# Decode attention beside a gated MLP: 28 rows of w_down summed by VectorE ahead of the last V

## The chip, the core and the metric

One NeuronCore of a Trainium2 chip runs the whole program. TensorE (PE) multiplies, VectorE (DVE) and ScalarE (ACT) work on tiles in SBUF and PSUM, GpSimd (POOL) makes two constants, and SyncE (SP) issues nearly all loads. The metric is the device time of one execution in microseconds; lower is better.

## The reference

One token passes through a block in which attention over a cache and a gated MLP stand side by side. The input x has 576 features, the cache 32 heads of 16384 positions with 128 features, the MLP 4608 inner features; all is in 32-bit floats.

```python
xn = _layernorm(x)
q = (xn @ wq)                                  # 32 heads of 128
scores = einsum("bhqd,bhkd->bhqk", q, k_cache) * (Dh ** -0.5)
o = einsum("bhqk,bhkd->bhqd", softmax(scores), v_cache)
attn = o.reshape(B, Sq, H * Dh) @ wo           # 4096 x 576
h = gelu(xn @ w_gate) * (xn @ w_up)            # tanh form of gelu
out = x + attn + h @ w_down                    # 4608 x 576
```

Each number of the caches and weights is used once. The caches alone are 2 x 32 x 8.39 MB.

## The kernel before

**Memory.** Three slots of SBUF, A, B and C, hold 64 KB in each of 128 partitions, so one slot takes one head's K or V (8.39 MB; a partition holds 128 positions). At the start the slots hold the weights w_q, w_gate and w_up. Later K of the even heads goes to B, K of the odd heads to A, and V of every head to C. At the end w_down (36 rows of 576 in each partition; "a row" below is 128 x 576 numbers) and w_o (32 such rows) go where room is.

**Order.** Nothing is scheduled by a planner: each engine's program is written out in order, and semaphores join them. `take(engine, s)` waits for a semaphore and lowers it, `give` raises it, `done` makes an engine wait for its own last instruction, and `load` issues a DMA. SP's loads all go to one queue, so a load that waits holds back every later one. fA, fB and fV tell SP that slot A, B or C is free; kA, kB and vL tell the engines that a K or V has landed.

**Stages.** First x is normed, and PE multiplies it with w_q, w_gate and w_up as they arrive; DVE and ACT make the MLP's inner vector hT from it. Then come 32 heads:
- `q_spread` on PE puts the head's q in all partitions; ACT copies it to `qs`.
- DVE (`dve_head`) multiplies the slot of K with qs in place (L188), sums over each 128 features into S (L191), and finds the largest score with PE's help (L193, L195, L370, L372). After L191 it frees the slot. L191 waits for `sf`, which PE gives with its first product on V of the head before, since S must have been read by then.
- ACT makes the exponentials `pe` (L264).
- PE multiplies pe with V in slot C (L377, 32 matmuls), ACT copies the result to `o4`, PE gathers it (L384) and with that frees slot C.

In one turn of SP's loop of heads, K for B, V, K for A and V are issued, each behind its slot's semaphore. Behind the loop the order is written out:

```python
        take(SP, fV)
        load(C, vv[H - 1], vL)
        take(SP, fB)
        load(B[:, : WD_A * D], wdv[:, : WD_A * D], s_tail[0])
        take(SP, fA)
        ...
```

that is V of the last head, 28 rows of w_down into B, its other 8 rows and 20 rows of w_o into A, and the last 12 rows of w_o in pieces of 6, 3, 2 and 1 into C.

**Tail.** `add_out` on PE (L401) adds one row after another into output banks: a row's 128 entries of hT or of the normed heads (`oT`) are the stationary operand, its 576 columns the moving one. Each row is two matmuls of 288 columns, and four of 144 for the last six rows. DVE clears the banks ahead of that (L335) and gives s_mz. After the row before the last six (s_hf) DVE adds the two halves' sums to x (L344, L345), PE adds that in (L429), and after the last row DVE copies the result (L347), which ACT stores.

Of the kernel before, what the change touches and what calls it, by code (L numbers as in the profile page):

```python
# [8 lines left out]
AF = mybir.ActivationFunctionType  # L9
ALU = mybir.AluOpType  # L10
AX = mybir.AxisListType

P = 128
H, SK, DH = 32, 16384, 128
D, DF = 576, 4608
R = SK // P
DJ = 4
DM = P * DJ
SCALE = DH**-0.5
EPS = 1e-5  # L20
HALF = D // 2
QUART = D // 4
# [3 lines left out]
WD_T = DF // P  # L26
FG = DF // 4
FB = (11 * WD_T, 11 * WD_T, 10 * WD_T)
WO_T = HD // P
ROW3 = 3 * DF  # L30
SLOT = R * DH
SLOTS = (28672, 94208, 159744)
LOW, HIGH = 16512, 225280
WD_A, WO_A = 28, 20
WO_C = (6, 3, 2, 1)
WO_Q = 6

# [2 lines left out]
def kernel(ctx: ExitStack, tc: tile.TileContext, x, k_cache, v_cache, wq, wo, wg, wu, wd, out):  # L40
    nc = tc.nc
    PE, DVE, ACT, SP, PL = nc.tensor, nc.vector, nc.scalar, nc.sync, nc.gpsimd
# [3 lines left out]
    def small(name, shape, where="low"):  # L46
        n = 4
        for s in shape[1:]:
            n *= s
        h = nc.alloc_sbuf_tensor_at(name, list(shape), F32, offset=at[where])  # L50
        at[where] += (n + 31) // 32 * 32
        assert at["low"] <= SLOTS[0] and at["high"] <= 229344
        return h.ap()
# [4 lines left out]
    A, B, C = slot("slot_a", 0), slot("slot_b", 1), slot("slot_c", 2)  # L58
# [3 lines left out]
    ones = small("ones", [P, P])  # L62
    x2 = small("x2", [P, HALF])
# [33 lines left out]
    onx = small("onx", [P, P])  # L97
    oT = small("oT", [P, WO_T])
    ot = small("ot", [P, QUART])

    kv = k_cache.rearrange("b h (p n) d -> (b h) p (n d)", p=P)
    vv = v_cache.rearrange("b h (p n) d -> (b h) p (n d)", p=P)
# [9 lines left out]
    def sem(name):  # L112
        return nc.alloc_semaphore(f"{name}_{next(count)}")
# [3 lines left out]
    def take(eng, s, n=1):  # L117
        eng.wait_ge(s, n).then_inc(s, -n)  # L118

    def give(eng, s, n=1):  # L120
        eng.sem_inc(s, n)

    def done(eng, inst):
        s = self_sem.setdefault(id(eng), None) or self_sem.__setitem__(id(eng), sem("own")) or self_sem[id(eng)]
        inst.then_inc(s, 1)
        take(eng, s)

    def load(dst, src, s, eng=None):
        (eng or SP).dma_start(dst, src).then_inc(s, 16)
# [7 lines left out]
    for n in "gu":  # L137
# [13 lines left out]
        sem(n) for n in ("qp", "qd", "qr", "pm", "pt", "nm", "pb", "ex", "sf", "pv", "o4", "pc"))  # L151
    s_al, s_pl, s_on, s_po, s_ot, s_mz, s_hf, s_x4, s_end, s_cp, s_out = (
        sem(n) for n in ("al", "pl", "on", "po", "ot", "mz", "hf", "x4", "end", "cp", "out"))
    s_tail = [sem("tail") for _ in range(3 + len(WO_C))]

    pgb = bank[:3]
    qgb = bank[3:5]
# [23 lines left out]
        take(PE, s_r)  # L181
        PE.matmul(pqb[:, :DH], ones, qh, start=True, stop=True).then_inc(qp, 1)  # L182

    def dve_head(k, slot, s_k, s_f):
        kt = slot.rearrange("p (n d) -> p n d", d=DH)
        take(DVE, s_k, 16)
        take(DVE, qr)
        done(DVE, DVE.tensor_mul(kt, kt, qs.unsqueeze(1).to_broadcast([P, R, DH])))  # L188
        give(DVE, qd)
        take(DVE, sf)  # L190
        done(DVE, DVE.tensor_reduce(S, kt, axis=AX.X, op=ALU.add))  # L191
        give(DVE, s_f)
        DVE.reduce_max(pm, S, axis=AX.X).then_inc(s_pm, 1)  # L193
        take(DVE, s_pt)
        DVE.tensor_reduce(nm, ptb[:1, :P], axis=AX.X, op=ALU.max, negate=True).then_inc(s_nm, 1)  # L195

    with tc.tile_critical(no_gpsimd_drain=True):

        load(wq_t, wmain["q"], s_wq)
        load(qt, wtail["q"], s_qt)  # L200
        for n in "gu":
            load(rows[n], wmain[n][:, ROW3:], s_mix[n])
# [2 lines left out]
        take(SP, fA)  # L205
        load(main["u"], wmain["u"][:, :ROW3], s_main["u"])
        take(SP, fB)
        load(B, kv[0], kB)
        take(SP, fA)
        load(A, kv[1], kA)  # L210
        take(SP, fV)
# [1 line left out]
        with SP.Fori(0, H // 2 - 1) as i:  # L213
            take(SP, fB)
            load(B, kv[bass.ds(2 * i + 2, 1)].rearrange("a p f -> (a p) f"), kB)
            take(SP, fV)
            load(C, vv[bass.ds(2 * i + 1, 1)].rearrange("a p f -> (a p) f"), vL)
            take(SP, fA)
            load(A, kv[bass.ds(2 * i + 3, 1)].rearrange("a p f -> (a p) f"), kA)
            take(SP, fV)  # L220
            load(C, vv[bass.ds(2 * i + 2, 1)].rearrange("a p f -> (a p) f"), vL)
        take(SP, fV)
        load(C, vv[H - 1], vL)
        take(SP, fB)
        load(B[:, : WD_A * D], wdv[:, : WD_A * D], s_tail[0])
        take(SP, fA)
        load(A[:, : (WD_T - WD_A) * D], wdv[:, WD_A * D :], s_tail[1])
        wo_a = (WD_T - WD_A) * D
        load(A[:, wo_a : wo_a + WO_A * D], wov[:, : WO_A * D], s_tail[2])
        take(SP, fV)  # L230
        lo = WO_A
        for k, n in enumerate(WO_C):
            load(C[:, (lo - WO_A) * D : (lo - WO_A + n) * D], wov[:, lo * D : (lo + n) * D], s_tail[3 + k])
            lo += n


        PL.memset(x2, 0.0).then_inc(s_zero, 1)
# [14 lines left out]
        done(ACT, ACT.activation(qs, pqb[:, :DH], AF.Copy))  # L252
        give(ACT, qr)
        give(ACT, s_q0)
        take(ACT, s_t1)
        ACT.activation(th, t1, AF.Tanh, scale=0.7978845608028654).then_inc(s_th, 1)
        with ACT.Fori(0, H) as h:
            q_pick(h + 1)
            take(ACT, qp)
            take(ACT, qd)  # L260
            ACT.activation(qs, pqb[:, :DH], AF.Copy).then_inc(qr, 1)
            take(ACT, s_pb)
            done(ACT, ACT.activation(nb, ptb[:, 256:257], AF.Copy, scale=SCALE))  # L263
            ACT.activation(pe, S, AF.Exp, bias=nb, scale=SCALE, accum_out=lsum[:, bass.ds(h, 1)]).then_inc(s_ex, 1)  # L264
            take(ACT, s_pv)
            ACT.activation(o4, PO, AF.Copy).then_inc(s_o4, 1)  # L266
            take(ACT, s_pc)
            done(ACT, ACT.activation(oall[:, bass.ds(h, 1)], pcb[:, :1], AF.Copy))
# [7 lines left out]
        done(DVE, DVE.memset(ones, 1.0))  # L276
        done(DVE, DVE.memset(eps_t, EPS))
        done(DVE, DVE.memset(whose[:, H:], 0.0))
        take(DVE, s_x, 16)
        for i in range(2):  # L280
            done(DVE, DVE.bn_stats(st[:, i, :], xrow[:, i * HALF : (i + 1) * HALF]))
# [46 lines left out]
        done(DVE, DVE.scalar_tensor_tensor(t2, th, 1.0, g, op0=ALU.add, op1=ALU.mult))  # L328
        done(DVE, DVE.scalar_tensor_tensor(hT, t2, 0.5, u, op0=ALU.mult, op1=ALU.mult))
        give(DVE, s_h)  # L330
        with DVE.Fori(0, H // 2):
            dve_head(0, B, kB, fB)
            dve_head(1, A, kA, fA)
        for z in (*half_b, bank[2]):
            done(DVE, DVE.memset(z, 0.0))  # L335
        give(DVE, s_mz)
# [26 lines left out]
            steps += [(j, main[n][:, j * DF : (j + 1) * DF], [(s_main[n], 16)] if j == 0 else []) for j in range(DJ - 1)]  # L363
            project(steps, FG, FB, pgb, s_pj)
        take(PE, s_q0)
        give(PE, sf)
        with PE.Fori(0, H):
            q_spread()
            take(PE, s_pm)
            PE.transpose(ptb[:1, :P], pm, ident).then_inc(s_pt, 1)  # L370
            take(PE, s_nm)
            PE.matmul(ptb[:, 256:257], ones[:1, :], nm, start=True, stop=True).then_inc(s_pb, 1)  # L372
            take(PE, s_ex)
            take(PE, vL, 16)
            for k in range(32):
                q = 32 * (k % 4)
                i = PE.matmul(PO[q : q + 4, :], pe[:, 4 * k : 4 * k + 4], C[:, k * 512 : (k + 1) * 512],  # L377
                              start=k < 4, stop=k >= 28)
                if k == 0:
                    i.then_inc(sf, 1)  # L380
            i.then_inc(s_pv, 1)
            take(PE, s_o4)
            for j in range(4):
                i = PE.matmul(pcb[:, :1], o4[:, j * DH : (j + 1) * DH], same[:, j : j + 1], start=j == 0, stop=j == 3)  # L384
                if j == 0:
                    i.then_inc(fV, 1)
            i.then_inc(s_pc, 1)
# [10 lines left out]
        def add_out(groups, lhs, w, last=False):  # L398
            n = D // len(groups)
            for k, gr in enumerate(groups):  # L400
                i = PE.matmul(gr, lhs, w[:, k * n : (k + 1) * n], start=id(gr) not in seen, stop=last)  # L401
                seen.add(id(gr))
            return i

        take(PE, s_tail[0], 16)
        for j in range(WD_A):
            add_out(half[j % 2], hT[:, j : j + 1], B[:, j * D : (j + 1) * D])
        take(PE, s_on)
        PE.matmul(bank[5][:, :WO_T], onx, same, start=True, stop=True).then_inc(s_po, 1)
        take(PE, s_tail[1], 16)  # L410
        for j in range(WD_A, WD_T):
            add_out(half[j % 2], hT[:, j : j + 1], A[:, (j - WD_A) * D : (j - WD_A + 1) * D])
        take(PE, s_ot)
        take(PE, s_tail[2], 16)
        ends = [sum(WO_C[:k]) + WO_A for k in range(len(WO_C))]
        for j in range(WO_T):
            if j in ends:
                take(PE, s_tail[3 + ends.index(j)], 16)
            w = A[:, wo_a + j * D : wo_a + (j + 1) * D] if j < WO_A else C[:, (j - WO_A) * D : (j - WO_A + 1) * D]
            if j < WO_T - WO_Q:  # L420
                i = add_out(half[j % 2], oT[:, j : j + 1], w, last=j >= WO_T - WO_Q - 2)
                if j == WO_T - WO_Q - 1:
                    i.then_inc(s_hf, 1)
                continue
            if j == WO_T - 3:
                take(PE, s_x4)
                for k, gr in enumerate(quart):
                    r, lo = 32 * (k // 2), k % 2 * QUART
                    PE.matmul(gr, ones[r : r + 1, :1], x2[r : r + 1, lo : lo + QUART], start=False, stop=False)  # L429
            i = add_out(quart, oT[:, j : j + 1], w, last=j == WO_T - 1)  # L430
        i.then_inc(s_end, 1)

        take(DVE, qr)
# [30 lines left out]
```

## Time and profile before

| | us |
|---|---|
| median of 3 runs | 1384.4 |
| all runs | 1384.4, 1381.16, 1564.85 |
| profiled execution, device time | 1383.64 |
| profiled execution, span of the trace | 1381.9 |
| busy: PE, DVE, ACT | 442.0, 1141.0, 71.5 |
| read from HBM | 587.60 MB, 425 GB/s over the span |

The span runs from the first to the last instruction that the trace shows; the device time is 1.74 us more. All times inside the execution are in microseconds from the start of the span. The longest of the three runs lies far from the other two, and the profiled execution lies with those two.

In the trace's rows, a timeline row has start, duration, engine, line, operation, tiles and count (matmuls that follow each other closely are merged into one row; a float matmul leaves two records), and in brackets the idle time of the engine before it. PEld is PE's load of the stationary operand. SPq and ACTq are the engines' issuing of DMAs. A row of stages gives its window and length, the busy time of PE, PEld, DVE, ACT and POOL with counts, the granted TensorE clock, the share of the DMA engines that was busy, and GB/s. The time from issue to landing is shown for each kind of load.

### The profile page before, as it was taken

Reading aid. Unit: us, or ns where it says so; the run is one execution under the profiler, and the core shown is the slowest. Engines: PE = TensorE matmul, PEld = TensorE weight load, DVE = VectorE, ACT = ScalarE, POOL = GpSimd, SP = SyncE. Lnnn points to the kernel's source line nnn. Section 1 sums busy time; section 2 is a strip of 40 time slices with the busy share of each in tenths; the row PEclk is TensorE's granted clock in tenths of the full one; section 3 lists DMA queues with packets and bytes.
Section 4 is the critical chain, followed back from the end, with each engine's and each line's share of the span. In section 5 each row is a group of like instructions: output and inputs, shape, how many; then the busy total and the mean of one; then the engine's idle time right before and its main releaser. Section 6 shows DMA issues by size and latency. Waiting matters only on the chain. (4 is left out here: it accounts for less than half of the span.)

```text
span 1381.9 us, 8013 instructions
## 1 busy us (share of the span) xinstructions
PE 442.0 (32%) x3104; PEld 171.5 (12%) x3104; DVE 1141.0 (83%) x173; ACT 71.5 (5%) x231; POOL 1.0 (0%) x7
## 2 busy tenths in 40 slices
PE   3531233333322233333332223333332223333336
PEld 1110011101110011111111011111110111111112
DVE  1149999999988998989888898989988899989910
ACT  0000000000000000000000000000000000000000
POOL 0000000000000000000000000000000000000000
PEclk9765565565555556556655665665665566566567
DMA  9999999999999999999999999999999999999697
GB/s 401 435 442 419 435 429 438 425 438 431 436 434 433 438 431 434 438 427 438 434 433 438 431 436 433 433 440 429 436 438 427 438 431 436 436 431 438 258 413 320
DMA packets 11396, 587.70 MB, mean 425 GB/s; under 512 B 1271, under 2 KB 1277, under 8 KB 1662
## 3 DMA queue, kind: packets, MB, share of 16 engines
q1 hardware_dynamic: 11376, 587.60, 98.4%
q8 instruction: 5, 0.08, 0.0%
q10 hardware_dynamic: 14, 0.01, 0.0%
q14 instruction: 1, 0.01, 0.0%
HBM read 587.60 MB, written 0.00 MB: 425 GB/s over the span
## 5 line engine op out<-in xcount | busy, mean ns | idle before, releaser
L377 PE MATMUL bank<-slot_c,pe 128*4 128x512 f32 x2048 | 296.4, 738 | 491.6 <-PEq L118 491.6
L191 DVE TENSOR_REDUCE s<-slot_a 128x128 f32<-128x16384 f32 x16 | 275.5, 17220 | 35.5 <-DVEq L118 35.5
L191 DVE TENSOR_REDUCE s<-slot_b 128x128 f32<-128x16384 f32 x16 | 275.5, 17220 | 31.5 <-DVEq L118 31.5
L188 DVE TENSOR_TENSOR slot_b<-slot_b,qs 128x16384 f32<-128x16384 f32 x16 | 275.6, 17225 | 8.4 <-DVEq L118 8.4
L188 DVE TENSOR_TENSOR slot_a<-slot_a,qs 128x16384 f32<-128x16384 f32 x16 | 275.6, 17226 | 0.0
L377 PEld LDWEIGHTS bank<-slot_c,pe 128*4 128x4 f32 x2048 | 84.7, 99 | 676.2 <-issue 664.5
L370 PE MATMUL bank<-ident,pm 128*1 128x128 f32 x32 | 11.9, 372 | 289.4 <-PEq L118 289.4
L266 ACT ACTIVATE o<-bank 128x512 f32<-128x512 f32 x32 | 19.1, 597 | 761.1 <-ACTq L118 761.1
L384 PE MATMUL bank<-same,o 128*128 128x1 f32 x256 | 32.7, 249 | 28.3 <-PEq L118 28.3
L370 PEld LDWEIGHTS bank<-ident,pm 128*1 128x1 f32 x32 | 2.5, 79 | 296.3 <-issue 296.3
L384 PEld LDWEIGHTS bank<-same,o 128*128 128x128 f32 x256 | 31.0, 191 | 57.1 <-issue 57.1
L182 PE MATMUL bank<-qh,ones 128*128 128x128 f32 x66 | 20.4, 402 | 54.6 <-PEq L118 54.6
L316 DVE TENSOR_TENSOR slot_c<-bank,same 128x396 f32<-128x396 f32 (+1 forms) x6 | 3.3, 558 | 37.1 <-DVEq L118 36.7
L344 DVE TENSOR_TENSOR x<-x,bank 64x288 f32<-64x288 f32 x1 | 0.5, 456 | 35.4 <-DVEq L118 35.4
L195 DVE TENSOR_REDUCE nm<-bank 1x1 f32<-1x128 f32 x32 | 8.9, 279 | 21.5 <-DVEq L118 21.5
L372 PE MATMUL bank<-nm,ones 1*128 1x1 f32 x64 | 17.7, 343 | 18.5 <-PEq L118 18.5
L303 DVE TENSOR_TENSOR slot_c<-bank,same 128x512 f32<-128x512 f32 x2 | 1.4, 692 | 26.1 <-DVEq L118 25.9
L263 ACT ACTIVATE nb<-bank 128x1 f32<-128x1 f32 x32 | 5.5, 171 | 303.3 <-ACTq L118 303.3
L182 PEld LDWEIGHTS bank<-qh,ones 128*128 128x128 f32 x66 | 13.3, 251 | 57.9 <-issue 57.9
L372 PEld LDWEIGHTS bank<-nm,ones 1*128 1x128 f32 x64 | 15.9, 307 | 27.9 <-issue 27.9
L338 DVE RECIPROCAL rl<-bank 128x32 f32<-128x32 f32 x1 | 0.4, 358 | 22.2 <-DVEq L118 22.2
L178 ACT ACTIVATE qh<-qd,whose 128x128 f32<-128x128 f32 x33 | 13.2, 401 | 49.3 <-ACTq L118 49.3
(77 smaller groups left out, 151.2 us busy)
## 6 DMA issues: line engine op xcount, KB each, us to landing
slot_b<-in_B_w_down_dram SPq DMA_DIRECT2D x1, 8064.0 KB, 40.5
slot_b<-in_B_w_gate_dram SPq DMA_DIRECT2D x1, 6912.0 KB, 55.4
slot_a<-in_B_w_up_dram SPq DMA_DIRECT2D x1, 6912.0 KB, 38.8
slot_a<-in_A_wo_dram SPq DMA_DIRECT2D x1, 5760.0 KB, 52.6
slot_c<-in_B_w_gate_dram SPq DMA_DIRECT2D x1, 2304.0 KB, 28.9
slot_c<-in_B_w_up_dram SPq DMA_DIRECT2D x1, 2304.0 KB, 36.0
slot_a<-in_B_w_down_dram SPq DMA_DIRECT2D x1, 2304.0 KB, 38.2
slot_c<-in_A_wo_dram SPq DMA_DIRECT2D x1, 1728.0 KB, 33.4
```

Source lines behind the costliest of these rows:

```text
L178: ACT.activation(qh, qd4.rearrange("p j t -> p (j t)"), AF.Copy, scale=whose[:, bass.ds(h, 1)]).then_inc(s_r, 1)
L182: PE.matmul(pqb[:, :DH], ones, qh, start=True, stop=True).then_inc(qp, 1)
L188: done(DVE, DVE.tensor_mul(kt, kt, qs.unsqueeze(1).to_broadcast([P, R, DH])))
L191: done(DVE, DVE.tensor_reduce(S, kt, axis=AX.X, op=ALU.add))
L195: DVE.tensor_reduce(nm, ptb[:1, :P], axis=AX.X, op=ALU.max, negate=True).then_inc(s_nm, 1)
L263: done(ACT, ACT.activation(nb, ptb[:, 256:257], AF.Copy, scale=SCALE))
L266: ACT.activation(o4, PO, AF.Copy).then_inc(s_o4, 1)
L316: done(DVE, DVE.tensor_mul(gm[:, at_ * WD_T : (at_ + m) * WD_T].rearrange("p (m t) -> p m t", t=WD_T), pgb[b][:, :size].rearrange("p (m t) ...
L370: PE.transpose(ptb[:1, :P], pm, ident).then_inc(s_pt, 1)
L372: PE.matmul(ptb[:, 256:257], ones[:1, :], nm, start=True, stop=True).then_inc(s_pb, 1)
L377: i = PE.matmul(PO[q : q + 4, :], pe[:, 4 * k : 4 * k + 4], C[:, k * 512 : (k + 1) * 512], start=k < 4, stop=k >= 28)
L384: i = PE.matmul(pcb[:, :1], o4[:, j * DH : (j + 1) * DH], same[:, j : j + 1], start=j == 0, stop=j == 3)
```

## The change

There are six edits.

1. `WD_B = 28` rows of w_down are loaded into slot B ahead of V of the last head, no longer behind it.
2. DVE, not PE, works on these rows: after its last head, a loop of 14 turns with two `scalar_tensor_tensor` each adds `B row x hT` to a new tile `acc` (128 x 576), each waiting for the one before. Then it gives `s_sum`, and only then does it clear the output banks and give s_mz. PE adds acc's partitions with one row's worth of matmuls against ones.
3. K of head 0 is loaded in two halves (semaphores `s_k0` and kB), and `dve_head` works on it in two parts. So that head stands ahead of DVE's loop, and the last head behind it.
4. `sf` comes from ACT, after it has made the exponentials, in place of PE's first matmul on V.
5. The first load, of w_q's main part, stands in a `tile_critical` section of its own, and all else in a second one.
6. The 20 rows of w_o in slot A come in pieces of 12 and 8, each with a semaphore; PE walks through a list `pieces`.

```diff
-WD_A, WO_A = 28, 20
+WD_B = 28
+WO_A = (12, 8)
...
+    acc = small("acc", [P, D])
...
+    pieces, at_a, lo = [(A, 0, wdv, WD_B, WD_T - WD_B)], WD_T - WD_B, 0
+    for n in WO_A:
+        pieces.append((A, at_a, wov, lo, n))
+        at_a, lo = at_a + n, lo + n
+    at_c = 0
+    for n in WO_C:
+        pieces.append((C, at_c, wov, lo, n))
+        at_c, lo = at_c + n, lo + n
...
-    def dve_head(k, slot, s_k, s_f):
+    def dve_head(slot, s_k, s_f, parts=1):
...
+        n = R // parts
+        for i in range(parts):
+            blk = kt[:, i * n : (i + 1) * n, :]
+            take(DVE, s_k if i == parts - 1 else s_k0, 16)
+            if i == 0:
+                take(DVE, qr)
+            done(DVE, DVE.tensor_mul(blk, blk, qs.unsqueeze(1).to_broadcast([P, n, DH])))
+            if i == parts - 1:
+                give(DVE, qd)
+            if i == 0:
+                take(DVE, sf)
+            done(DVE, DVE.tensor_reduce(S[:, i * n : (i + 1) * n], blk, axis=AX.X, op=ALU.add))
...
     with tc.tile_critical(no_gpsimd_drain=True):
-
         load(wq_t, wmain["q"], s_wq)
+    with tc.tile_critical(no_gpsimd_drain=True):
+
         load(qt, wtail["q"], s_qt)
...
-            load(B, kv[0], kB)
+            for half_k in range(2):
+                k0 = slice(half_k * SLOT // 2, (half_k + 1) * SLOT // 2)
+                load(B[:, k0], kv[0][:, k0], (s_k0, kB)[half_k])
...
+        take(SP, fB)
+        load(B[:, : WD_B * D], wdv[:, : WD_B * D], s_wd)
         take(SP, fV)
         load(C, vv[H - 1], vL)
-        take(SP, fB)
-        load(B[:, : WD_A * D], wdv[:, : WD_A * D], s_tail[0])
         take(SP, fA)
...
         give(ACT, s_q0)
+        give(ACT, sf)
...
-            ACT.activation(pe, S, AF.Exp, bias=nb, scale=SCALE, accum_out=lsum[:, bass.ds(h, 1)]).then_inc(s_ex, 1)
+            done(ACT, ACT.activation(pe, S, AF.Exp, bias=nb, scale=SCALE, accum_out=lsum[:, bass.ds(h, 1)]))
+            give(ACT, s_ex)
+            give(ACT, sf)
...
+        done(DVE, DVE.memset(acc, 0.0))
...
-        with DVE.Fori(0, H // 2):
-            dve_head(0, B, kB, fB)
-            dve_head(1, A, kA, fA)
+        dve_head(B, kB, fB, 2)
+        with DVE.Fori(0, H // 2 - 1):
+            dve_head(A, kA, fA)
+            dve_head(B, kB, fB)
+        dve_head(A, kA, fA)
+        take(DVE, s_wd, 16)
+        with DVE.Fori(0, WD_B // 2) as i:
+            for k in range(2):
+                done(DVE, DVE.scalar_tensor_tensor(acc, B[:, bass.ds((2 * i + k) * D, D)], hT[:, bass.ds(2 * i + k, 1)], acc,
+                                                   op0=ALU.mult, op1=ALU.add))
+        give(DVE, s_sum)
...
-        give(PE, sf)
...
-                if k == 0:
-                    i.then_inc(sf, 1)
...
+        take(PE, s_sum)
+        add_out(half[1], ones[:, :1], acc)
         take(PE, s_tail[0], 16)
-        for j in range(WD_A):
-            add_out(half[j % 2], hT[:, j : j + 1], B[:, j * D : (j + 1) * D])
+        for j in range(WD_B, WD_T):
+            add_out(half[j % 2], hT[:, j : j + 1], A[:, (j - WD_B) * D : (j - WD_B + 1) * D])
```

SP's program behind its loop of heads, before (slot_c from the V cache is V of the last head):

```order
L129 DMA slot_c<-in_A_v_cache_dram 128x16384
L129 DMA slot_b<-in_B_w_down_dram 128x16128
L129 DMA slot_a<-in_B_w_down_dram 128x4608
L129 DMA slot_a<-in_A_wo_dram 128x11520
L129 DMA slot_c<-in_A_wo_dram 128x3456
```

and SP's program at the same place now:

```order
L131 DMA slot_b<-in_B_w_down_dram 128x16128
L131 DMA slot_c<-in_A_v_cache_dram 128x16384
L131 DMA slot_a<-in_B_w_down_dram 128x4608
L131 DMA slot_a<-in_A_wo_dram 128x6912
L131 DMA slot_a<-in_A_wo_dram 128x4608
L131 DMA slot_c<-in_A_wo_dram 128x3456
```

The load into slot B has moved ahead of V, and w_o's load into slot A has become two.

DVE behind the last head, before (nm is the last head's largest score, bank are the output banks, rl, on and onx norm the heads' outputs):

```order
L195 TENSOR_REDUCE nm<-bank 1x1
L331 REGISTER_ALU
L331 COMPARE_AND_BRANCH
L335 MEMSET bank 128x512 x3
L338 RECIPROCAL rl<-bank 128x32
L339 TENSOR_TENSOR on<-oall,rl 128x32
L340 TENSOR_TENSOR onx<-on,quarter 128x128
```

and DVE at the same place now (ISA rows make addresses from the loop's count):

```order
L212 TENSOR_REDUCE nm<-bank 1x1
L358 UNCONDITIONAL_BRANCH
L358 ISA
L360 REGISTER_ALU
L360 SCALAR_TENSOR_TENSOR acc<-slot_b,hT,acc 128x576
L360 ISA
L360 SCALAR_TENSOR_TENSOR acc<-slot_b,hT,acc 128x576
L358 REGISTER_ALU
L358 COMPARE_AND_BRANCH
L364 MEMSET bank 128x512 x3
L367 RECIPROCAL rl<-bank 128x32
L368 TENSOR_TENSOR on<-oall,rl 128x32
```

The loop over acc stands between the last head and the memsets, so the memsets and the three operations of the norm are behind it.

SP's program at its start now:

```order
L214 NO_OP
L482 UNCONDITIONAL_BRANCH
L131 DMA slot_a<-in_A_wq_dram 128x16384
L214 UNCONDITIONAL_BRANCH
L214 NO_OP
L216 NO_OP
L482 UNCONDITIONAL_BRANCH
L131 DMA slot_b<-in_A_wq_dram 128x2048
```

The first load has the same rows in front of it as before; the four rows behind it, up to the second load, are new.

More of the change, by code (lines that the diff above doesn't have):

```diff
@@ L153 @@
         sem(n) for n in ("al", "pl", "on", "po", "ot", "mz", "hf", "x4", "end", "cp", "out"))
-    s_tail = [sem("tail") for _ in range(3 + len(WO_C))]
+    pieces, at_a, lo = [(A, 0, wdv, WD_B, WD_T - WD_B)], WD_T - WD_B, 0
[6 more added lines that the diff above has]
+        at_c, lo = at_c + n, lo + n
+    s_tail = [sem("tail") for _ in pieces]
+    s_wd, s_sum, s_k0 = sem("wd"), sem("sum"), sem("k0")
     pgb = bank[:3]
@@ L182, in q_spread @@
         PE.matmul(pqb[:, :DH], ones, qh, start=True, stop=True).then_inc(qp, 1)
-    def dve_head(k, slot, s_k, s_f):
+    def dve_head(slot, s_k, s_f, parts=1):
         kt = slot.rearrange("p (n d) -> p n d", d=DH)
[L186 to L191, printed above, removed]
+        n = R // parts
[10 more added lines that the diff above has]
+            done(DVE, DVE.tensor_reduce(S[:, i * n : (i + 1) * n], blk, axis=AX.X, op=ALU.add))
         give(DVE, s_f)
@@ L221 @@
             load(C, vv[bass.ds(2 * i + 2, 1)].rearrange("a p f -> (a p) f"), vL)
+        take(SP, fB)
+        load(B[:, : WD_B * D], wdv[:, : WD_B * D], s_wd)
         take(SP, fV)
         load(C, vv[H - 1], vL)
-        take(SP, fB)
-        load(B[:, : WD_A * D], wdv[:, : WD_A * D], s_tail[0])
         take(SP, fA)
-        load(A[:, : (WD_T - WD_A) * D], wdv[:, WD_A * D :], s_tail[1])
-        wo_a = (WD_T - WD_A) * D
-        load(A[:, wo_a : wo_a + WO_A * D], wov[:, : WO_A * D], s_tail[2])
+        for (t, to, src, lo, n), sm in zip(pieces[:-len(WO_C)], s_tail):
+            load(t[:, to * D : (to + n) * D], src[:, lo * D : (lo + n) * D], sm)
         take(SP, fV)
[L231 to L234, printed above, removed]
+        for (t, to, src, lo, n), sm in list(zip(pieces, s_tail))[-len(WO_C):]:
+            load(t[:, to * D : (to + n) * D], src[:, lo * D : (lo + n) * D], sm)
         PL.memset(x2, 0.0).then_inc(s_zero, 1)
@@ L403, in add_out @@
             return i
+        take(PE, s_sum)
+        add_out(half[1], ones[:, :1], acc)
         take(PE, s_tail[0], 16)
-        for j in range(WD_A):
-            add_out(half[j % 2], hT[:, j : j + 1], B[:, j * D : (j + 1) * D])
+        for j in range(WD_B, WD_T):
+            add_out(half[j % 2], hT[:, j : j + 1], A[:, (j - WD_B) * D : (j - WD_B + 1) * D])
         take(PE, s_on)
         PE.matmul(bank[5][:, :WO_T], onx, same, start=True, stop=True).then_inc(s_po, 1)
-        take(PE, s_tail[1], 16)
@@ L411 @@
-        for j in range(WD_A, WD_T):
-            add_out(half[j % 2], hT[:, j : j + 1], A[:, (j - WD_A) * D : (j - WD_A + 1) * D])
         take(PE, s_ot)
[L414 to L430, printed above, removed]
+        for (t, to, _, lo, n), sm in list(zip(pieces, s_tail))[1:]:
+            take(PE, sm, 16)
+            for j in range(lo, lo + n):
+                w = t[:, (to + j - lo) * D : (to + j - lo + 1) * D]
+                if j < WO_T - WO_Q:
+                    i = add_out(half[j % 2], oT[:, j : j + 1], w, last=j >= WO_T - WO_Q - 2)
+                    if j == WO_T - WO_Q - 1:
+                        i.then_inc(s_hf, 1)
+                    continue
+                if j == WO_T - 3:
+                    take(PE, s_x4)
+                    for k, gr in enumerate(quart):
+                        r, c = 32 * (k // 2), k % 2 * QUART
+                        PE.matmul(gr, ones[r : r + 1, :1], x2[r : r + 1, c : c + QUART], start=False, stop=False)
+                i = add_out(quart, oT[:, j : j + 1], w, last=j == WO_T - 1)
```

## The prediction

> **What bounds the kernel now.** I read the page first: the span, the slices, the queues.
>
> ```profile
> span 1381.9 us, 8013 instructions
> ...
> DMA  9999999999999999999999999999999999999697
> GB/s 401 435 442 419 435 429 438 425 438 431 436 434 433 438 431 434 438 427 438 434 433 438 431 436 433 433 440 429 436 438 427 438 431 436 436 431 438 258 413 320
> ...
> q8 instruction: 5, 0.08, 0.0%
> ```
>
> The transfers are busy in every slice but the 38th and the 40th. So the kernel is bound by its reads, and only those two slices can give much back. The table of stages puts numbers on this.
>
> ```profile
> 140.00:1291.00 1151.00, 348.07 (x2282) 136.69 (x2274) 1056.05 (x121) 63.42 (x210) 0.00 (x0) 0.61 1.00 434
> 1291.00:1306.00 15.00, 10.79 (x72) 4.12 (x72) 12.32 (x2) 0.60 (x1) 0.00 (x0) 0.70 0.05 22
> 1306.00:1375.00 69.00, 31.53 (x323) 11.03 (x327) 10.44 (x9) 2.48 (x9) 0.00 (x0) 0.68 0.97 413
> 1375.00:1381.90 6.90, 2.81 (x72) 1.31 (x60) 1.21 (x3) 0.00 (x0) 0.00 (x0) 1.00 0.00 0
> ```
>
> The last column is GB/s: 434 for 1151 us, then a hole of 15 us at 22, then 413, then 6.9 us with nothing to read. The timeline shows what makes the hole and the end (first number: start; second: duration).
>
> ```profile
> 1236.70 0.33 SPq L129 DMA_DIRECT2D slot_a<-in_A_k_cache_dram  x1
> ...
> 1255.76 8.69 PE L377 MATMUL bank<-slot_c,pe 128*4 128x512 f32 x64 [17.27 <-PEq L118]
> ...
> 1257.77 17.22 DVE L191 TENSOR_REDUCE s<-slot_b 128x128 f32<-128x16384 f32 x1 [2.51 <-DVEq L118]
> ...
> 1275.23 0.29 DVE L193 TENSOR_REDUCE pm<-s 128x1 f32<-128x128 f32 x1 [0.24 <-DVEq L118]
> ...
> 1276.45 17.23 DVE L188 TENSOR_TENSOR slot_a<-slot_a,qs 128x16384 f32<-128x16384 f32 x1
> ...
> 1294.34 9.98 PE L377 MATMUL bank<-slot_c,pe 128*4 128x512 f32 x64 [17.18 <-PEq L118]
> ...
> 1296.36 17.22 DVE L191 TENSOR_REDUCE s<-slot_a 128x128 f32<-128x16384 f32 x1 [2.68 <-DVEq L118]
> ...
> 1306.10 0.36 SPq L129 DMA_DIRECT2D slot_b<-in_B_w_down_dram  x1
> ...
> 1315.94 0.48 DVE L335 MEMSET bank<- 128x512 f32 x1 [0.29 <-DVEq L118]
> ...
> 1327.63 8.60 PE L377 MATMUL bank<-slot_c,pe 128*4 128x512 f32 x64 [11.87 <-PEq L118]
> ...
> 1337.58 1.79 SPq L129 DMA_DIRECT2D slot_c<-in_A_wo_dram  x4
> ...
> 1340.28 0.29 DVE L340 TENSOR_TENSOR onx<-on,quarter 128x128 f32<-128x128 f32 x1
> ...
> 1346.69 9.21 PE L401 MATMUL bank<-slot_b,hT 128*1 128x288 f32 x112 [7.40 <-PEq L118]
> ...
> 1356.17 2.12 PE L401 MATMUL bank<-slot_a,hT 128*1 128x288 f32 x32
> ...
> 1366.98 7.37 PE L401 MATMUL bank<-slot_a,oT 128*1 128x288 f32 x80 [8.69 <-PEq L118]
> ...
> 1375.99 0.46 DVE L344 TENSOR_TENSOR x<-x,bank 64x288 f32<-64x288 f32 x1 [35.42 <-DVEq L118]
> ...
> 1377.19 0.42 PE L429 MATMUL bank<-x,ones 1*1 1x144 f32 x8 [0.65 <-PEq L118]
> ...
> 1377.54 0.92 PE L401 MATMUL bank<-slot_c,oT 128*1 128x144 f32 x24
> ```
>
> V of head 30 is seen by PE at 1294.34, V of head 31 can be issued only when PE is through with slot C, and w_down's first load stands behind it on SP, issued at 1306.10. But slot B, where w_down goes, was free since the reduce of 1257.77 ended at 1274.99. So SP held back a load that had its place, and the transfers ran dry.
>
> At the end, the 20 rows of w_o arrive as one piece at 1366.98 and cost PE 7.37, so PE is still at them when the last small pieces land:
>
> ```profile
> slot_c<-in_A_wo_dram SPq DMA_DIRECT2D x1, 288.0 KB, 36.3
> ...
> slot_a<-in_A_k_cache_dram SPq DMA_DIRECT2D x16, 38.2
> ```
>
> The last of the four issues that end at 1339.37 starts near 1338.9; with 36.3 it lands at 1375.2, 6.7 before the span ends.
>
> **The change, part by part.**
>
> *w_down ahead of the last V.* SP now issues those 28 rows when slot B is free (1275 at the latest), while V of head 30 is on its way. They fill the hole; V of head 31, issued just ahead of 1306.10 as before, queues behind them. The hole is 15.00 x (1 - 22/434) = 14.2 us. The wait for slot A and its loads stand behind V on SP as before. By landings the same comes out: V of head 30 at 1294.3, 28 rows in 19.0 (1327.63 to 1346.69) at 1313.3, V of head 31 in 19.3 (half of 1255.76 to 1294.34) at 1332.6, and the rest as before, 1375.2 - 1346.7 = 28.5, at 1361.1. That is 14.1 earlier. What is late next: the pieces in slot C are issued after V of head 31 is used, 1337.6 - 1327.6 = 10 after it lands, at 1342.6; the loads for slot A keep the queue full until about 1352, so no second hole.
>
> *DVE sums the 28 rows.* PE loses 9.21 us that lay beside the transfers. DVE gains 28 multiply-adds of 128x576, each waiting for the one before, in a loop of 14 turns. No row has this operation at this size. The nearest:
>
> ```profile
> L303 DVE TENSOR_TENSOR slot_c<-bank,same 128x512 f32<-128x512 f32 x2 | 1.4, 692 | 26.1 <-DVEq L118 25.9
> ...
> 87.34 0.20 DVE L324 TENSOR_TENSOR t<-gu 128x36 f32<-128x36 f32 x1 [0.24 <-DVEq L118]
> ...
> 87.69 0.18 DVE L325 TENSOR_SCALAR t<-t 128x36 f32<-128x36 f32 x1
> ...
> 90.34 0.20 DVE L329 SCALAR_TENSOR_TENSOR hT<-t,gu 128x36 f32<-128x36 f32 x1
> ...
> 1238.04 17.22 DVE L188 TENSOR_TENSOR slot_b<-slot_b,qs 128x16384 f32<-128x16384 f32 x1 [0.25 <-DVEq L118]
> ```
>
> At 36 elements this operation costs what a product costs (0.20), so I take a product's price at 576: 0.692 + 64 x 17.22/16384 = 0.76. A dependent successor starts 0.15 after (87.54 to 87.69), a turn of a loop adds 0.25 (the idle time at 1238.04), and I allow 0.06 for the computed addresses. A turn is 2 x 0.76 + 2 x 0.15 + 0.25 + 0.06 = 2.13; 14 turns are 29.8. Bounds: 2 x 0.76 + 0.25 = 1.8 a turn (25 us in all) if the addresses are made during the operation before, 3.0 (42 us) if each operation waits 0.6 more; the rows lie near the lower. The sum runs from 1313.3 to 1343.1.
>
> Behind it on DVE now stand the three memsets of the output banks, once hidden at 1315: 3 x 0.48 + 2 x 0.29 = 2.0, with the signal 2.3. The three operations that then norm the heads' outputs ended with the row at 1340.28, 12.7 after V of head 31 landed; that would be 1345.3 now, and they wait about 1 us. PE needs them only after eight rows of w_down. PE waits for the sum and the memsets in front of all its remaining rows: 0.5 for the sum's own matmuls (one slow row); 3.8 for eight rows of w_down at the slow 0.48 (the 9.21 of the row at 1346.69 are 28 rows, of which about eight must have been slow if the others took the quick 2.12/8 = 0.27 of the row at 1356.17); 0.8 for two small steps on PE and ACT before w_o; 5.3 for 20 quick rows, 1.6 for six; then DVE's two additions and PE's restart 1.2 (1375.99 to 1377.19), 0.4 + 0.9, and 3.4 from the last matmul (1378.46) to the end. With the 2.3: 20.2. So the chain over DVE ends at 1343.1 + 20.2 = 1363.3.
>
> Does a long operation hold its successor longer than a short one? The reduce of 17.22 that ends at 1274.99 is followed 0.24 later (1275.23), the products of 0.20 after 0.15. The Trainium skill says otherwise ("VectorE: DVE Perf Modes", section "The DRAIN you can't avoid"): behind each operation stands a flush of about its duration less 266 ns. Added to my rows that would be 0.5 for each multiply-add, 14 us for the sum, and a time near 1379 in place of 1367. The trace does not agree: by that rule the 17.22 would be followed by 17.
>
> *Smaller last pieces.* With 12 and 8 rows PE does the first piece while the second is on its way, and is no longer late for the last landing. The end then is the last landing plus one row (0.92/3 = 0.3), 0.3 of signals and 3.4: 4.0 in place of 6.7, a gain of 2.7. The extra issue on SP (0.4) lies beside V of head 31. The chain over the transfers ends at 1361.1 + 4.0 = 1365.1, 1.8 after that over DVE: the sum is just hidden.
>
> *The reduce no longer waits for PE's first product* but for ACT's exponential, which is early. DVE sheds the 2.51 and 2.68 per head. What is late next is K: head 31's lands at 1236.70 + 38.2 = 1274.9, so DVE is done at about 1311 and slot A comes free at 1309.7, both ahead of need. V comes behind K on a full queue, so the pace stays at 38.58 a head: nothing at the end.
>
> *First section, first head.*
>
> ```profile
> 0.96 0.34 POOL L237 MEMSET x<- 128x288 f32 x1 [0.51 <-SPq L197]
> 0.97 0.39 SPq L129 DMA_DIRECT2D slot_a<-in_A_wq_dram  x1
> ...
> 25.42 3.64 PE L173 MATMUL bank<-slot_b,xtb 128*32 128x512 f32 x16 [15.87 <-PEq L118]
> ...
> 95.23 17.23 DVE L188 TENSOR_TENSOR slot_b<-slot_b,qs 128x16384 f32<-128x16384 f32 x1 [4.70 <-DVEq L118]
> ...
> 130.45 0.34 SPq L129 DMA_DIRECT2D slot_b<-in_A_k_cache_dram  x1
> ```
>
> The same three rows of SP stand in front of the first load, so I take 0; it can gain 0.5 at most (the section's entry, the POOL row) or lose as much. The other engines enter a second section some 0.5 to 1 later, and DVE clears the new sum (0.7): both lie in PE's idle 15.87, and the other early loads queue behind w_q. In halves, K's first head lets DVE start at 90.5 instead of 95.23 and free slot B at 125.8 instead of 130.4; V of head 0 was on the way until about 131, so that gains 0 to 0.5. I take 0.
>
> **Sum.** 1381.9 - 14.1 - 2.7 = 1365.1 span. The profiled execution took 1383.64, 1.74 over its span: 1366.9, say 1367, 1.3% under the median of 1384.4 (the profiled execution lay 0.8 under that median).
>
> **Rivals.**
> 1. *The sum is late.* From 1344.9 on (2.26 a turn) each microsecond of it shows at the end. At the 3.0 of the upper bound it ends at 1355.3, the span at 1375.5, the time is 1377. For it: no row shows computed addresses on DVE. Against: the rows above. One way to it is that each multiply-add holds the next for most of its own time; two thirds of 0.76 is 0.5, 14 us in all, 1379. The row at 1275.23 leaves little for that, 0.02 of the 0.13 below. It is what the page's flush would do.
> 2. *Slower: each turn of DVE's loop fetches its instructions anew.* The nearest rows to a small fetch are x's load and its first use:
>
> ```profile
> 0.93 0.54 ACTq L129 DMA_DIRECT2D slot_c<-in_A_x_dram  x1
> ...
> 2.38 1.04 DVE L281 BATCH_NORM_STATS2 st<-slot_c 1x6 f32<-1x288 f32 x2 [0.69 <-DVEq L118]
> ```
>
>    That is 1.45. Fourteen of these, 20.3, put the end at 1383.6 and the time at 1385; from 1.4 a turn it is slower than the median before. Against: five instruction packets on that queue in the whole run, though DVE's loop turns 16 times. The Trainium skill has the rule ("Runtime: NRT & Kernel Launch", section "Instruction fetch mechanics"): a taken branch to a place outside the two pages at hand forces a fetch. No row here shows one.
> 3. *The hole only moves.* If slot B came free late, or the pieces in slot C were issued late, up to 14.2 would come back: 1381. Against: 30 us of slack for the first, 9 for the second.
> 4. *Faster: the freed DVE and the earlier requests raise the pace.* 440 in place of 434 over the 32 heads is 1.4% of 1235, 17 us: 1350. Against: the queue was never empty in that stage (434 over 1151 us, share 1.00).
>
> **How the numbers follow.** Forecast, 1363 to 1370: 0.74. Late sum, 1370 to 1382: 0.13. Loop fetch: 0.04, half of it over 2% slower. Hole moved: 0.04. Faster pace: 0.05. A measurement of this kernel tells about 2% from no change; 2% below 1384.4 is 1356.7, above it 1412.1. So faster 0.05, same 0.93, slower 0.02. The range starts at 1362 (both half-microsecond gains of the start and a little more at the seam) and reaches to 1375, into the late sum to 2.8 a turn; outside are 0.05 below and about 0.13 above.
>
> **What would show it.** Right: no stage near 1291 to 1306 without reads; DVE's multiply-adds from about 1313 to 1343, some 0.76 each and 2.1 a turn; V of head 31 seen at 1332 to 1333; PE idle before its last rows and 4 us from the last landing to the end. Reduces of K without idle time and products of K waiting for K. Wrong: PE working without a pause from the sum to the end (rival 1 or 2), a new stretch at 0 GB/s (rival 3), or a pace other than 38.6 a head (rival 4, or a slower one).

## The result and the profile after

| | before | changed |
|---|---|---|
| median, us | 1383.26 (4 runs) | 1370.88 (4 runs, 1370.62 to 1371.44) |
| ratio to before, 95% interval | | 0.9916, 0.9897 to 0.9936 |
| profiled execution, us | 1383.64 | 1371.0 |
| its span, us | 1381.9 | 1368.4 |

The changed kernel takes 0.84% less time. The interval of the ratio lies wholly below 1, so the gain is clear of the noise, but it is smaller than the 2% that the prediction took as the border of "same". The forecast was 1367, range 1362 to 1375: 3.9 too low, inside the range. (One execution of the kernel before, 1564.85, lies far above the others; it is counted in the median of 4 and left out of the ratio.)

From the page of the changed kernel, span, slices of 34 us and the queue of instructions (q8):

```profile
span 1368.4 us, 8040 instructions
...
DMA  9999999999999999999999999999999999999996
GB/s 399 445 428 448 428 431 431 433 433 448 429 431 431 433 433 448 429 431 431 433 433 448 429 431 431 433 433 448 429 431 431 433 433 448 429 431 431 431 430 282
...
q8 instruction: 5, 0.08, 0.0%
```

The low 38th slice is gone; only the last one is still low. The stages of the changed kernel (last column GB/s):

```profile
140.00:1291.00 1151.00, 348.07 (x2282) 141.35 (x2274) 1055.18 (x121) 63.37 (x210) 0.00 (x0) 0.61 1.00 434
1291.00:1306.00 15.00, 10.21 (x74) 4.25 (x74) 14.65 (x2) 1.45 (x4) 0.00 (x0) 0.82 0.99 430
1306.00:1357.00 51.00, 18.44 (x135) 8.28 (x139) 28.38 (x37) 1.63 (x6) 0.00 (x0) 0.60 0.98 419
1357.00:1368.40 11.40, 7.39 (x148) 3.38 (x136) 1.21 (x3) 0.00 (x0) 0.00 (x0) 0.98 0.03 11
```

Where 22 GB/s stood, 430 stand now. But reads end near 1357, and 11.4 us without them follow, against 6.9 before. The timeline of the changed kernel shows what runs in these:

```profile
1293.00 8.73 PE L405 MATMUL bank<-slot_c,pe 128*4 128x512 f32 x64 [20.90 <-PEq L120]
...
1303.04 0.34 SPq L131 DMA_DIRECT2D slot_c<-in_A_v_cache_dram  x1
...
1312.29 0.82 DVE L360 SCALAR_TENSOR_TENSOR acc<-slot_b,hT,acc 128x576 f32<-128x576 f32 x1 [2.23 <-DVEq L120]
1313.41 0.82 DVE L360 SCALAR_TENSOR_TENSOR acc<-slot_b,hT,acc 128x576 f32<-128x576 f32 x1 [0.30 <-DVEq L120]
1314.87 0.82 DVE L360 SCALAR_TENSOR_TENSOR acc<-slot_b,hT,acc 128x576 f32<-128x576 f32 x1 [0.64 <-DVEq L120]
...
1331.33 10.04 PE L405 MATMUL bank<-slot_c,pe 128*4 128x512 f32 x64 [20.57 <-PEq L120]
...
1342.68 1.75 SPq L131 DMA_DIRECT2D slot_c<-in_A_wo_dram  x4
...
1346.63 0.82 DVE L360 SCALAR_TENSOR_TENSOR acc<-slot_b,hT,acc 128x576 f32<-128x576 f32 x1 [0.28 <-DVEq L120]
1348.00 0.48 DVE L364 MEMSET bank<- 128x512 f32 x1 [0.55 <-DVEq L120]
...
1350.49 0.65 PE L427 MATMUL bank<-acc,ones 128*1 128x288 f32 x2 [5.92 <-PEq L120]
...
1355.90 5.03 PE L427 MATMUL bank<-slot_a,oT 128*1 128x288 f32 x80 [0.61 <-PEq L120]
1360.75 2.37 PE L427 MATMUL bank<-slot_c,oT 128*1 128x288 f32 x48
...
1364.11 0.92 PE L427 MATMUL bank<-slot_c,oT 128*1 128x144 f32 x24
```

The sum on DVE ends at 1347.45. PE stands still for 5.92 until the sum and the memsets are done (1350.49), and from there works nearly without a pause to the end. The last small piece had landed more than 5 us before PE's last rows, which begin at 1364.11:

```profile
slot_c<-in_A_wo_dram SPq DMA_DIRECT2D x1, 288.0 KB, 14.6
```

Its issue began near 1344.0 (the four end at 1344.43, one takes 0.4), and it took 14.6, so it landed at 1358.6, 9.8 before the span's end; the prediction gave 4.0 for that stretch. This looks like the first rival, the late sum.

### The profile page after: what moved, and what is told of

It reads as the page before. It is cut to its first block, busy times and chain, and to the rows that moved or that the text cites. A ratio compares the mean times of both kernels' runs of the same rounds, so it can differ in the third digit from the quotient of the medians.

```text
span 1368.4 us, 8040 instructions
## 1 busy us (share of the span) xinstructions
PE 432.4 (32%) x2996; PEld 175.4 (13%) x2996; DVE 1165.0 (85%) x204; ACT 71.5 (5%) x231; POOL 1.0 (0%) x7
## 5 line engine op out<-in xcount | busy, mean ns | idle before, releaser
L203 DVE TENSOR_TENSOR slot_a<-slot_a,qs 128x16384 f32<-128x16384 f32 x16 | 275.6, 17225 | 29.9 <-DVEq L120 29.8
L203 DVE TENSOR_TENSOR slot_b<-slot_b,qs 128x16384 f32<-128x16384 f32 (+1 forms) x17 | 275.8, 16221 | 28.9 <-DVEq L120 28.9
L208 DVE TENSOR_REDUCE s<-slot_b 128x128 f32<-128x16384 f32 (+1 forms) x17 | 275.7, 16216 | 5.7 <-DVEq L120 5.7
L405 PEld LDWEIGHTS bank<-slot_c,pe 128*4 128x4 f32 x2048 | 91.0, 99 | 786.5 <-issue 775.5
L360 DVE SCALAR_TENSOR_TENSOR acc<-slot_b,hT,acc 128x576 f32<-128x576 f32 x28 | 22.9, 819 | 14.5 <-DVEq L120 14.5
L210 DVE TENSOR_REDUCE pm<-s 128x1 f32<-128x128 f32 x32 | 9.2, 286 | 7.6 <-DVEq L120 7.6
```

Of the source, the lines that this page charges most:

```text
L203: done(DVE, DVE.tensor_mul(blk, blk, qs.unsqueeze(1).to_broadcast([P, n, DH])))
L208: done(DVE, DVE.tensor_reduce(S[:, i * n : (i + 1) * n], blk, axis=AX.X, op=ALU.add))
L360: done(DVE, DVE.scalar_tensor_tensor(acc, B[:, bass.ds((2 * i + k) * D, D)], hT[:, bass.ds(2 * i + k, 1)], acc, op0=ALU.mult, op1=ALU.add))
```

## The experiments

The experiments ask three things: is the sum what ends last, which edit carries the gain, and what do the small edits bring.

**1. The sum without its loop.** From here on "written out" means this edit.

```diff
-        with DVE.Fori(0, WD_B // 2) as i:
-            for k in range(2):
-                done(DVE, DVE.scalar_tensor_tensor(acc, B[:, bass.ds((2 * i + k) * D, D)], hT[:, bass.ds(2 * i + k, 1)], acc,
-                                                   op0=ALU.mult, op1=ALU.add))
+        for j in range(WD_B):
+            done(DVE, DVE.scalar_tensor_tensor(acc, B[:, j * D : (j + 1) * D], hT[:, j : j + 1], acc, op0=ALU.mult, op1=ALU.add))
```

> The changed kernel with its 28 multiply-adds written out instead of a loop of 14 turns. Theory 1 (the loop's computed addresses and its turn make the sum late, and the sum's end sets the end): one row costs 0.82 + 0.15 = 0.97, the sum takes 27 us instead of 35 and ends near 1339.5; then the transfers end last (last landing 1358.6 + 4.0), span near 1362.6, 5.8 less than the changed kernel, time near 1365. Theory 2 (a dependent multiply-add waits 0.28 whatever its addresses): a row costs 1.10, the sum ends near 1343, span near 1364. Theory 3 (the sum is hidden, something behind the last landing is late): span stays at 1368.4.

Measured: 1366.26 (4 runs), ratio 0.9871 (0.9854 to 0.9887), whose interval lies below the changed kernel's; span 1363.3, against 1368.4. Its timeline:

```profile
1311.81 0.82 DVE L359 SCALAR_TENSOR_TENSOR acc<-slot_b,hT,acc 128x576 f32<-128x576 f32 x1 [1.92 <-DVEq L120]
1312.79 18.20 DVE L359 SCALAR_TENSOR_TENSOR acc<-slot_b,hT,acc 128x576 f32<-128x576 f32 x19 [0.16 <-DVEq L120]
...
1331.51 7.58 DVE L359 SCALAR_TENSOR_TENSOR acc<-slot_b,hT,acc 128x576 f32<-128x576 f32 x8 [0.52 <-DVEq L120]
...
1350.63 2.12 PE L425 MATMUL bank<-slot_a,oT 128*1 128x288 f32 x32 [0.47 <-PEq L120]
1354.72 3.68 PE L425 MATMUL bank<-slot_c,oT 128*1 128x288 f32 x48 [1.97 <-PEq L120]
```

A row costs 0.97 with some 0.15 to its successor (0.16 behind the first row, one longer wait of 0.52), the sum ends at 1339.1, and PE now waits for pieces (the 0.47 and 1.97). So theory 1 holds: in the changed kernel the loop's turns are on the path, in this one the transfers end last. Theories 2 and 3 fall.

**2. More turns.** One multiply-add a turn, 28 turns.

```diff
-        with DVE.Fori(0, WD_B // 2) as i:
-            for k in range(2):
-                done(DVE, DVE.scalar_tensor_tensor(acc, B[:, bass.ds((2 * i + k) * D, D)], hT[:, bass.ds(2 * i + k, 1)], acc,
-                                                   op0=ALU.mult, op1=ALU.add))
+        with DVE.Fori(0, WD_B) as i:
+            done(DVE, DVE.scalar_tensor_tensor(acc, B[:, bass.ds(i * D, D)], hT[:, bass.ds(i, 1)], acc,
+                                               op0=ALU.mult, op1=ALU.add))
```

> The changed kernel with one multiply-add per turn, 28 turns. Theory 1: each row has the turn's 0.63 behind it, 1.45 a row, 40.6 for the sum, which ends near 1353; span 5.4 longer, near 1373.8, time near 1376. Theory 3: no change, 1368.4.

Measured: 1373.49, ratio 0.9925 (0.9908 to 0.9941), span 1371.6, 3.2 more than the changed kernel. Two rows of its timeline:

```profile
1313.63 0.82 DVE L359 SCALAR_TENSOR_TENSOR acc<-slot_b,hT,acc 128x576 f32<-128x576 f32 x1 [0.55 <-DVEq L120]
1314.99 0.82 DVE L359 SCALAR_TENSOR_TENSOR acc<-slot_b,hT,acc 128x576 f32<-128x576 f32 x1 [0.54 <-DVEq L120]
```

A turn with one row leaves 0.55 idle, not the 0.63 of a turn with two, so the sum grew by 2.4 (the memsets behind it start at 1350.43 instead of 1348.00), where 5.4 was expected. Direction as theory 1 says; the price of a turn was set too high.

**3. Clearing the banks first.** The three memsets and `give(DVE, s_mz)` stand ahead of `take(DVE, s_wd, 16)`.

> The changed kernel with the three memsets of the output banks, and their signal, ahead of the sum, in DVE's wait for the 28 rows. Theory 1: the chain behind the sum loses 2.3, and what the memsets push back in front of it is 0 to 0.4 (DVE waits 2.2 there); span 1366.1 to 1366.6. Theory 3: 1368.4.

Measured: 1369.50, ratio 0.9897 (0.9881 to 0.9914), spans 1366.0 to 1367.0 in four executions, against 1368.1 to 1368.9: 1.4 less in the profiled ones. The sum began 0.6 later (1312.90), and PE took up its rows at 1348.52 instead of 1350.49. One span lies just below the 1366.1 to 1366.6 that was expected, three lie 0.2 to 0.4 above it. So the memsets behind the sum were on the path.

**4. One section again.**

```diff
         load(wq_t, wmain["q"], s_wq)
-    with tc.tile_critical(no_gpsimd_drain=True):
-
         load(qt, wtail["q"], s_qt)
```

> The changed kernel in one section as before the change. The time lay 1.74 over the span before the change and 2.6 over it after. If the second section costs that: 2.6 goes back to about 1.75, the span stays within 0.4, the time is near 1370.1 instead of 1371. If it comes from something else (longer program of DVE): 2.6 stays. In both cases x's load lands 1.5 after its issue again, in place of 8.7, since it no longer stands behind the first load; PE's first projection still starts near 25.4.

Measured: 1371.54 (1370.32 to 1372.91), ratio 0.9909 (0.9892 to 0.9925): not to be told from the changed kernel. The span of the profiled execution was 1370.8, 2.4 more than the changed kernel's: PE began its 20 rows of w_o 0.8 later (1356.67) and took 6.62 for them instead of 5.03 (in the stage from 1358 to 1364 the granted clock was 0.84, against 1.00); the other three spans were 1368.1 to 1369.4. The time over the span was 2.1 to 2.9, so that question stays open (below). x's load is quick again: bn_stats starts at 2.79, against 10.59.

**5. The load's place alone, on the kernel before.**

```diff
+        take(SP, fB)
+        load(B[:, : WD_A * D], wdv[:, : WD_A * D], s_tail[0])
         take(SP, fV)
         load(C, vv[H - 1], vL)
-        take(SP, fB)
-        load(B[:, : WD_A * D], wdv[:, : WD_A * D], s_tail[0])
```

> The kernel before with one edit: the load of 28 rows of w_down into slot B stands ahead of V of the last head. PE adds these rows as before, behind its last head. If the place of the load carries the gain: no hole, V of head 31 seen near 1332.6, PE free for the 28 rows at 1344.5, 8.5 for these, 2.1 for eight, 0.8, 5.3 for 20, 1.6 for six, 1.2 + 1.3 + 3.4 to the end: span near 1368.4, no worse than the changed kernel. If the move of the sum to DVE is needed for it (PE's 28 rows then come cold, 9.2 to 13): span 1369 to 1374. If the load ahead of V is worth nothing: 1381.9.

Measured: 1368.79 (5 runs, 1367.65 to 1376.96), ratio 0.9911 (0.9884 to 0.9938), spans 1365.7 to 1369.5 in four executions and 1375.2 in one. Two lines moved give as much as the whole change. The timeline of the profiled execution, span 1369.5:

```profile
1275.83 0.34 SPq L129 DMA_DIRECT2D slot_b<-in_B_w_down_dram  x1
...
1333.33 9.84 PE L377 MATMUL bank<-slot_c,pe 128*4 128x512 f32 x64 [16.93 <-PEq L118]
...
1346.46 8.32 PE L401 MATMUL bank<-slot_b,hT 128*1 128x288 f32 x112
...
1355.04 2.12 PE L401 MATMUL bank<-slot_a,hT 128*1 128x288 f32 x32
...
1356.98 5.03 PE L401 MATMUL bank<-slot_a,oT 128*1 128x288 f32 x80
```

V of head 31 is seen at 1333.33, and PE then works through all rows without a pause: here PE ends last, as DVE does in the changed kernel.

**6. K's first head whole**, on the kernel with the sum written out (one `load(B, kv[0], kB)`, and `dve_head(B, kB, fB)`).

> The changed kernel with the 28 multiply-adds written out (as in the first experiment, so that the transfers end last), and K of head 0 loaded and worked on whole again. The changed kernel saw V of head 30 at 1293.0, the kernel before at 1294.3. If the halves made that: V of head 1 at 173.3 instead of 172.5 and of head 30 at 1294.3, the span 1.3 longer than with halves, near 1364.6. If ACT's signal for the reduce made it: 1293.0 and 1363.3 stay.

Measured: 1368.42, ratio 0.9899 (0.9882 to 0.9915), spans 1364.8 to 1366.0 against 1362.8 to 1363.3 with halves (experiment 1). From its timeline, K of head 2 is issued at 130.33, and V of head 1 seen at:

```profile
174.25 6.15 PE L401 MATMUL bank<-slot_c,pe 128*4 128x512 f32 x36 [5.83 <-PEq L120]
...
1294.92 8.54 PE L401 MATMUL bank<-slot_c,pe 128*4 128x512 f32 x64 [20.88 <-PEq L120]
```

and in the changed kernel, with halves:

```profile
126.62 0.35 SPq L131 DMA_DIRECT2D slot_b<-in_A_k_cache_dram  x1
...
172.51 3.00 PE L405 MATMUL bank<-slot_c,pe 128*4 128x512 f32 x12 [7.80 <-PEq L120]
```

So the halves bring 1.7 at head 1, and that is still there at head 30 (1294.92 against 1293.00). From 126 to 150 this kernel reads 416 GB/s and the changed one 438, which is 1.2 us of reading. That fits a request for K of head 2 that came too late, although it stood ahead of the landing of V of head 0: PE saw that V 3.3 after the request here (133.59), and 7.3 after it in the changed kernel (133.91). No run moves the request without halving the load.

**7. The reduce waits for PE again**, on the kernel with the sum written out (`give(PE, sf)` and the signal of PE's first product as before the change).

> The changed kernel with the 28 multiply-adds written out, and the reduce waiting for PE's first product on V again. DVE's reduces wait 2.5 a head for V, the last head's ends near 1312.5 instead of 1308.6, the sum starts 2 to 3 later and ends near 1342, still hidden: if the signal is worth nothing at the end, the span stays within 0.5 of 1363.3. If the signal carried the 1.3 of the heads' stage, V of head 30 comes at 1294.3 and the span at 1364.6. Theory 3 of a pace set by DVE: more than 2 longer.

Measured: 1364.97, ratio 0.9874 (0.9857 to 0.9890), span 1363.0, V of head 30 at 1292.82. ACT's signal is worth nothing in the span, and the halves alone made the gain of the heads' stage.

**8. The 20 rows in one piece**, on the kernel with the sum written out (`WO_A = (20,)`).

> The changed kernel with the 28 multiply-adds written out and the 20 rows of w_o in slot A in one piece again. They land near 1350 and PE, idle since 1346.6 and so cold, takes 5.3 to 7.4 for them: the six rows behind them end at 1357 to 1359 instead of 1357, the span is 1363.3 to 1365.3. If the split were worth the 2.7 that the prediction gave to the last pieces: 1366.

Measured: 1367.27, ratio 0.9890 (0.9873 to 0.9906), spans 1364.8 to 1365.8, so the split brings 1.5 to 3 of span where the sum is not in the way. From its timeline:

```profile
1350.62 6.64 PE L425 MATMUL bank<-slot_a,oT 128*1 128x288 f32 x80 [2.01 <-PEq L120]
1357.09 2.36 PE L425 MATMUL bank<-slot_c,oT 128*1 128x288 f32 x48
```

PE waits 2.01 for the piece and then is late for the last ones.

**9. All rows on PE**, in the changed kernel: no loop on DVE, and PE adds the 28 rows behind its last head. On PE's side:

```diff
-        take(PE, s_sum)
-        add_out(half[1], ones[:, :1], acc)
+        take(PE, s_wd, 16)
+        for j in range(WD_B):
+            add_out(half[j % 2], hT[:, j : j + 1], B[:, j * D : (j + 1) * D])
```

> The changed kernel without its sum on DVE: PE adds the 28 rows itself, behind its last head; loads, halves, sections and pieces as in the changed kernel. With the order alone the span ended 36.2 after V of head 31 was seen, PE working without a pause; V is seen at 1331.3 here: span near 1367.5. Then the sum on DVE, in its loop, costs about 1 instead of bringing something, and only written out (1363.3) it brings 4. If moving the rows off PE brought a gain even in the loop: over 1370.

Measured: 1369.72, ratio 0.9912 (0.9895 to 0.9928), spans 1365.9 to 1368.2. By the ratios it can't be told from the changed kernel, by the spans it is 0 to 3 better. The 28 rows cost PE 6.97 in the profiled execution (8.32 in experiment 5), and what PE waits for the loop on DVE in the changed kernel costs about the same.

**10. What was left standing, together**: sum written out, halves, load ahead of V, pieces of 12 and 8, the reduce waiting for PE as before, one section.

> What the runs so far leave standing, together: the multiply-adds written out, K of head 0 in halves, the load ahead of V, the pieces of 12 and 8; the reduce waiting for PE's product as before the change, and one section. Transfers end last: span 1363.0, as with two sections. The time lies 1.9 to 2.2 over the span if one section gives that always, so 1365; 2.5 to 3.3, so 1366, if the section has no part in it.

Measured: 1364.75 (4 runs, 1364.66 to 1365.32), ratio 0.9875 (0.9858 to 0.9891), spans 1362.7 to 1363.4. It beats the kernel before and the changed one; against the kernels of experiments 1 and 7 it makes no clear difference.

## Why the prediction was right, and where it was off

**The hole.** Right. 28 rows ahead of V filled it (430 GB/s where 22 stood), V of head 31 was seen at 1331.33 (forecast 1332.6), and the place of the load alone gives the whole gain of the change (experiment 5).

**The sum.** Here a term was mis-sized, and with it the order of the two chains: the forecast was added up along the transfers, and the chain over DVE, 1.8 below them in the forecast, ended last. The prediction took a turn of the loop at 2.13; it was 2.56:

| per turn of two rows | forecast | measured |
|---|---|---|
| the two operations | 2 x 0.76 | 2 x 0.82 |
| between the two | 0.15 + 0.03 | 0.28 |
| to the next turn | 0.15 + 0.25 + 0.03 | 0.63 |

Written out, a successor starts after 0.15, as the old rows had it. What was missing is mainly what computed addresses add: 0.13 inside a turn, and with the turn itself 0.48 between turns, against the 0.28 allowed for edge and addresses. The 0.25 came from a turn of the loop of heads, whose slots have fixed addresses. The sum took 35.2 instead of 29.8 (28 x 0.06 = 1.7 of that is the operation, the rest the waits) and ended at 1347.45 instead of 1343.1; the threshold that the first rival named (2.26 a turn, 1344.9) was passed. The chain behind it was forecast at 20.2 and took 20.95, which puts the end at 1368.4. Rival 1 is what happened, at a price between the likeliest value and the upper bound of 3.0; its chance of 0.13 was too low for a forecast with a margin of 1.8. The time lies in its band (1370 to 1382). The range held it because it reached into that band. That 1367 itself came near is in part luck, since it was added up along a chain that was not the one that ended last.

**The chain over the transfers** was forecast to end at 1365.1. It isn't seen in the changed kernel, but with the sum written out it ends at 1363.3: 1.8 earlier, mostly by the halves, which were taken as 0, bound 0.5, and bring 1.9 by V of head 30 (experiment 6). The step that failed is that V of head 0 "was on the way until about 131", so that a request at 130.4 would be in time. V of head 0 was on the way longer: in the changed kernel, where ACT's exponentials were ready at 129.4, PE saw it at 133.91. The request at 126.62 gained 1.7 over the one at 130.33.

**Small pieces.** The forecast gave them 2.7. In the changed kernel they could bring nothing, since PE came to them after they had landed; where the transfers end last the split brings 1.5 to 3 (experiment 8).

**The reduce's signal, the section.** Both were taken as 0 at the end, and no run shows other than 0 in the span (experiments 7 and 4). DVE's reduces do run at once, and its products wait for K (2.34 and 2.39 idle ahead of the products at 1235.13 and 1273.79), as forecast. The late start of the other engines did lie in PE's idle time, but that cover shrank from 15.87 to 7.62, since x's load came late by a way that was not foreseen (below).

**Time over span.** The forecast kept 1.74; the changed kernel lies 2.52 to 2.6 over its span. That is 0.8 of the 4.1 by which the profiled execution (1371.0) lies above the forecast's 1366.9; the other 3.3 is the span, 1368.4 in place of 1365.1. The cause of the 0.8 stays open: over the runs the time over the span was 1.9 to 2.0 in four executions of experiment 10, 2.1 to 2.9 with one section and the loop (4), 2.2 to 3.3 written out with two sections (1), so neither the section nor the loop sets it alone.

**Flush and fetch.** No flush of a length like the operation's shows: in experiment 1 an operation of 0.82 is followed after some 0.15. The rule of the Trainium skill ("VectorE: DVE Perf Modes", section "The DRAIN you can't avoid") would ask for 0.55, an estimate from its duration less 266 ns; the trace does not agree. Nor does the fetch of rival 2 show: five packets of instructions as before, and 0.55 to 0.64 between turns, where the rival had 1.45.

## What to carry to other kernels

Before work is moved to another engine, look at the order of the queue: here a load that stood behind a wait which it didn't need was the whole gain, and two moved lines gave it. When work is moved into a loop on another engine, price the turn with its computed addresses from a loop of that engine, or write it out; and where two chains end within 2 us of each other, say how far the earlier one may slip before it is the one that ends last. Ask early for the next block: here a request some 3 us before the block under way was seen seems to have come too late, while one 7 us before gained 1.7.

## What was not expected of the hardware

x's load, 2.2 KB issued from ACT, took 1.45 from issue to use before the change (0.93 to 2.38) and 8.66 after (1.93 to 10.59), although it is on another queue than w_q's load. It was issued 1.0 behind w_q's 8.39 MB, where before it had left 0.04 ahead. With one section again (experiment 4) it is used at 2.79. The rows of the changed kernel:

```profile
0.97 0.38 SPq L131 DMA_DIRECT2D slot_a<-in_A_wq_dram  x1
...
1.93 0.52 ACTq L131 DMA_DIRECT2D slot_c<-in_A_x_dram  x1
...
10.59 1.04 DVE L302 BATCH_NORM_STATS2 st<-slot_c 1x6 f32<-1x288 f32 x2 [7.05 <-DVEq L120]
```

That the one load stands behind the packets of the other fits all three runs; that it is the packets on the same DMA engines was not tested by itself.

The same multiply-add leaves 0.15, 0.28 or 0.63 idle behind it on DVE: with fixed addresses, with computed ones, and at a loop's turn with computed ones. And the same 20 rows of w_o on PE took 5.03, 6.62 or 6.64 by the granted clock during them: 1.00 throughout in the changed kernel; 0.50 until 1358 and 0.84 in the 6 us behind that in experiment 4; 0.50 until 1353 and 0.88 from there to 1357 in experiment 8. That moves a tail that PE ends by 1.6. The kernels of the first two differ only in the section at the start; what sets the moment at which the clock rises is not shown.
